# One value load of each turn issued as two loads by ranges of its rows, in a cached attention block

## The chip, the cores and the metric

The kernel runs on one core of a Trainium2 chip. The metric is the device time of one execution in microseconds (us).

## What is computed

The reference projects x to queries, attends to a cache of keys and values for every batch and head, and projects the result back. Everything is bfloat16.

```python
B, Sq, D = 8, 112, 640
H, Sk, Dh = 32, 512, 192
q = (x @ wq).reshape(B, Sq, H, Dh).transpose(0, 2, 1, 3)
scores = jnp.einsum("bhqd,bhkd->bhqk", q, k_cache) * (Dh ** -0.5)
p = softmax(scores, axis=-1)
o = jnp.einsum("bhqk,bhkd->bhqd", p, v_cache)
return o.transpose(0, 2, 1, 3).reshape(B, Sq, H * Dh) @ wo
```

## The kernel before

The work is cut into 16 turns, t = 0 to 15. A turn is one batch and one half of the heads (16 of 32): turns 0 to 7 are the first half, 8 to 15 the second. A turn has 4 steps of 4 heads each, so there are 64 steps, n = 4t + s. In step n TensorE (PE) computes the scores of n (lines 368 to 383), then the product of probabilities and values of step n - 2 (lines 459 and 470), pieces of the projection of a later batch (line 313) and of the output projection of an earlier one (line 504), and the transposes of the probabilities of step n - 1 (line 431). VectorE (DVE) takes the row maximum and the normalisation, ScalarE (ACT) the exponential and the evacuations of PSUM. The order on each engine is written out by hand in lists; a small planner (`Plan`) turns the named dependencies into waits on counting semaphores. A consumer of an operation with several semaphores waits for each of them.

All loads are issued by SyncE (SP), on one queue, in this order from turn 3 on: K(t), V(t-1, 8), in some turns a weight, V(t, 0), then K(t+1) and so on.

- `load_k` (line 143, issue at 150) loads the keys of a turn with one transposing DMA into one of two buffers, kt. It waits until the scores of turn t - 2 are done.
- `load_v` (line 157, issue at 165) loads the values of 8 heads: V(t, 0) for the heads of steps 0 and 1 of the turn, V(t, 8) for those of steps 2 and 3. One load has 128 rows, one for each partition of SBUF; a row is 8 heads of 1,536 bytes. It waits until the values that lay in its buffer have been used (`PVm`, line 470). From turn 2 on V(t, 0) goes to buffer vt1 and V(t, 8) to vt0, but for the last.
- The weights: `load_wo` (208) for the output projection in turns 2 and 3 (first half) and 10 and 11 (second half), `load_wq` (198) for the second half of the query projection in turns 5 to 8. The weight of w_of[t] stands between V(t-1, 8) and V(t, 0).

In the source, the first matmul of step n that reads the values is named `PVt` (line 464); it depends on the transposed probabilities and on the value load. The four PVt of a turn read V(t, 0) twice, then V(t, 8) twice.

Of the kernel before, what the change touches and what calls it, by code (L numbers as in the profile page):

```python
# [11 lines left out]
class Plan:  # L12
# [7 lines left out]
    def add(self, eng, name, deps, emit, sem=None, inc=1):  # L20
        assert name not in self.ops, name
        self.ops[name] = dict(eng=eng, deps=deps, emit=emit, sem=sem or eng, inc=inc)
# [30 lines left out]
def build_mha_kernel(nc, x, k_cache, v_cache, wq, wo, out):  # L53
# [16 lines left out]
    def place(n):  # L70

        return divmod(n, 4)
# [3 lines left out]
    for n in range(NN):  # L76
        t, s = place(n)
# [3 lines left out]
    with ExitStack() as es:  # L81
# [42 lines left out]
        add, order = P.add, P.order  # L124
# [6 lines left out]
        v_home = [0, 1, 2] + [i % 2 for i in range(3, len(v_units))]  # L131
# [3 lines left out]
        def v_tile(i):  # L135
            return {2: vx, 3: v_late}[v_home[i]] if v_home[i] > 1 else vt[v_home[i]]

        def v_free(i):

            old = [j for j in range(i) if v_home[j] == v_home[i]]  # L140
            return [step_of[v_units[old[-1]][0], 2 * v_units[old[-1]][1] + j] for j in range(2)] if old else []

        def load_k(t, lo, hi):
# [10 lines left out]
            for s in range(lo // 4, hi // 4):  # L154
                k_piece[t, s] = name

        def load_v(t, lo, hi):
            half, b = divmod(t, B)
            i = v_units.index((t, lo // 8))
            name = ("V", t, lo)  # L160
            deps = [("PVm", n, 1) for n in v_free(i)] + {2: [("KT", HU - 1)], 3: [("Qb", NM - 1, LP - 1)]}.get(v_home[i], [])

            def emit(e):
                src = v_cache[b, half * HU + lo:half * HU + hi].rearrange("u (r q) d -> r u (q d)", q=4)
                return e.dma_start(v_tile(i)[:, lo % 8:lo % 8 + hi - lo, :], src)
            add("SP", name, deps, emit, f"mV{v_home[i]}", 16)
            order["SP"].append(name)
            for s in range(lo // 4, hi // 4):
                v_piece[t, s] = name
# [51 lines left out]
        load_kn(8, 16)  # L221
        load_wq(0, 6)
        load_v(0, 0, 8)
        load_x(1, 2, 4)
        load_x(2, 4, 7)
        load_v(0, 8, 16)
        load_k(1, 0, HU)
        load_v(1, 0, 8)
        load_k(2, 0, HU)
        load_v(1, 8, 16)  # L230
# [617 lines left out]
def bass_standalone__mha_block_cached__near_ridge_kernel(  # L848
    nc: bass.Bass,
    x: bass.AP,  # L850
    k_cache: bass.AP,
    v_cache: bass.AP,
    wq: bass.AP,
    wo: bass.AP,
    out: bass.AP,
):
    return build_mha_kernel(nc, x, k_cache, v_cache, wq, wo, out)
# [28 lines left out]
```

## Time and profile before

| | us |
|---|---|
| time, two runs | 456.86 and 459.51, median 458.19 |
| span of the profiled execution | 456.1 |
| TensorE matmuls busy | 432.3 (95%) |
| VectorE busy | 364.6 (80%) |
| ScalarE busy | 334.1 (73%) |
| value load, median from issue to landing (30 loads, 1,536 KB each) | 8.6 |
| key load, the same (15 transposes) | 24.6 |
| wo load, the same (4 loads, 1,920 KB each) | 13.0 |

The profile is of one execution. "Busy" is the time in which an engine has an instruction at work; "idle before" is the time in which it waited, with the releaser that came last. PE is TensorE's matmuls, PEld its weight loads, SPq the instructions of SP, which are issues of DMAs: their duration is the time that SP needs to hand the DMA to the queue, not the time of the transfer. The transfers run on 16 DMA engines; "to landing" is the time from the issue to the last of their completions. Lines such as L165 are lines of the kernel.

### The profile page before, as it was taken

The numbers are of one execution on the slowest core, as the hardware profiler recorded it, in microseconds if no ns is written. First come the engines' busy times: TensorE is split into PE (matmuls) and PEld (weight loads), VectorE is DVE, ScalarE is ACT, GpSimd is POOL, SyncE is SP. The second block draws the span as 40 slices with busy tenths as digits, with TensorE's granted clock in tenths as the row PEclk, the third lists the DMA queues.
The fourth block names the chain that finished last, engine by engine and source line by source line (L and its number), as shares of the span: only waits on it lengthen the run. The fifth ranks groups of instructions, "written<-read, shape, count | busy, mean of one in ns | idle before, by whom it ended". The sixth has DMA issues, their size and how long they took to land.

```text
span 456.1 us, 14769 instructions
## 1 busy us (share of the span) xinstructions
PE 432.3 (95%) x6227; PEld 398.1 (87%) x6227; DVE 364.6 (80%) x1160; ACT 334.1 (73%) x782; POOL 0.7 (0%) x6
## 2 busy tenths in 40 slices
PE   5788999999979999999999999997999999999996
PEld 4777888989979899999999999996999999999996
DVE  0577799888868989888888888886688888889971
ACT  3668799867857777877687768776577687767783
POOL 0000000000000000000000000000000000000000
PEclk9999999999999999999999999998899999999999
DMA  8999999999999999999999999999989999999972
GB/s 266 373 363 202 284 244 374 216 314 313 245 317 230 345 230 316 243 293 276 253 319 239 315 228 334 282 235 367 226 225 262 261 213 250 270 225 251 225 204 64
DMA packets 243442, 121.93 MB, mean 267 GB/s; under 512 B 194864, under 2 KB 243376, under 8 KB 243376
## 3 DMA queue, kind: packets, MB, share of 16 engines
q1 hardware_dynamic: 243376, 120.99, 110.0%
q8 instruction: 49, 0.80, 0.7%
q14 instruction: 17, 0.14, 0.1%
HBM read 70.35 MB, written 1.15 MB: 157 GB/s over the span
## 4 chain that ended last, share of the span: by engine, by line
PE 79%; ACT 10%; DMA 6%; DVE 5%; issue 0%; SPq 0%; DVEq 0%
PE ps L504 17%; PE ps L313 16%; PE ps L470 10%; PE ps L431 9%; PE ps L381 7%; ACT p_sb L401 6%; PE ps L459 6%; PE ps L368 6%; PE ps L370 5%; DMA wo_sb<-in_wo_dram 3%; DVE s_sb L396 2%; DMA vt<-in_v_cache_dram 2%; PE ps L543 1%; ACT oT_sb L480 1%; PE ps L567 1%; DVE p_sb L405 1%
## 5 line engine op out<-in xcount | busy, mean ns | idle before, releaser
L401 ACT ACTIVATE p_sb<-s_sb,nmx 112x512 bf16<-112x512 f32 x256 | 182.4, 713 | 83.8 <-DVE s_sb L396 81.8
L396 DVE TENSOR_SCALAR_CACHE_REDUCE s_sb<-ps 112x512 f32<-112x512 f32 x256 | 167.2, 687 | 42.5 <-ACT p_sb L401 20.0
L313 PE MATMUL ps<-xT_sb,wq_sb 128*128 128x224 bf16 x960 | 111.4, 262 | 1.3 <-ACT xT_sb L278 1.3
L504 PE MATMUL ps<-oT_sb,wo_sb 128*128 128x224 bf16 x840 | 97.7, 261 | 3.3 <-DMA wo_sb<-in_wo_dram 3.3
L313 PEld LDWEIGHTS ps<-xT_sb,wq_sb 128*128 128x128 bf16 x960 | 90.2, 99 | 2.8 <-DMA wq_sb<-in_wq_dram 1.1
L405 DVE TENSOR_SCALAR p_sb<-p_sb,rinv 112x512 bf16<-112x512 bf16 x256 | 79.0, 350 | 4.4
L504 PEld LDWEIGHTS ps<-oT_sb,wo_sb 128*128 128x128 bf16 x840 | 78.8, 98 | 3.9 <-DMA wo_sb<-in_wo_dram 3.6
L319 ACT ACTIVATE qr<-ps 128x448 bf16<-128x448 f32 (+1 forms) x112 | 48.9, 441 | 16.1 <-PE ps L313 16.0
L431 PE MATMUL ps<-ident,p_sb 112*128 112x112 bf16 x944 | 57.2, 214 | 1.9 <-ACT oT_sb L480 1.9
L437 ACT ACTIVATE pT_sb<-ps 128x896 bf16<-128x896 bf16 x59 | 53.3, 903 | 4.4 <-PE ps L431 3.7
L431 PEld LDWEIGHTS ps<-ident,p_sb 112*128 112x128 bf16 x944 | 52.0, 99 | 4.1 <-ACT oT_sb L480 4.1
L470 PE MATMUL ps<-pT_sb,vt 128*128 128x112 bf16 x880 | 52.8, 213 | 0.0
L480 ACT ACTIVATE oT_sb<-ps 128x672 bf16<-128x672 f32 x64 | 45.4, 710 | 6.0 <-PE ps L470 6.0
L401 ACT ACTIVATION_READ_ACCUMULATOR p_sb<-s_sb,nmx 112x1 f32 x256 | 48.4, 189 | 0.0
L470 PEld LDWEIGHTS ps<-pT_sb,vt 128*128 128x128 bf16 x880 | 44.1, 98 | 4.3
L437 DVE COPY pT_sb<-ps 128x896 bf16<-128x896 bf16 x59 | 36.4, 616 | 9.1 <-PE ps L431 9.0
L459 PEld LDWEIGHTS ps<-pT_sb,vt 128*64 128x64 bf16 x880 | 24.0, 109 | 14.2 <-issue 9.5
L459 PE MATMUL ps<-pT_sb,vt 128*64 128x112 bf16 x880 | 32.1, 216 | 4.2 <-DVE s_sb L396 2.4
L370 PE MATMUL ps<-kt,qh 128*112 128x256 bf16 x128 | 35.2, 275 | 0.0
L368 PE MATMUL ps<-kt,qh 128*112 128x256 bf16 x128 | 35.1, 274 | 0.0
L368 PE MATMUL ps<-kt,qr 128*112 128x256 bf16 x112 | 31.0, 277 | 3.8 <-DVE qh L346 2.3
L383 PE MATMUL ps<-kt,qh 64*112 64x256 bf16 x128 | 34.0, 291 | 0.0
(70 smaller groups left out, 481.3 us busy)
## 6 DMA issues: line engine op xcount, KB each, us to landing
vt<-in_v_cache_dram SPq DMA_DIRECT2D x30, 1536.0 KB, 8.6
wo_sb<-in_wo_dram SPq DMA_DIRECT2D x4, 1920.0 KB, 13.0
wq_sb<-in_wq_dram SPq DMA_DIRECT2D x7, 960.0 KB, 11.2
wo_sb<-in_k_cache_dram SPq DMA_DIRECT2D x2, 768.0 KB, 10.2
wo_sb<-in_k_cache_dram SPq DMA_DIRECT2D x1, 1536.0 KB, 15.0
wo_sb<-in_v_cache_dram SPq DMA_DIRECT2D x1, 1536.0 KB, 7.8
wq_sb<-in_v_cache_dram SPq DMA_DIRECT2D x1, 1536.0 KB, 8.1
out_dram<-xT_sb SPq DMA_DIRECT2D x8, 140.0 KB, 2.3
```

The lines of the kernel that those rows point to most:

```text
L313: mm = e.matmul(ps[:, bank, j * S2:(j + 1) * S2], wq_sb[:, dc, c0:c0 + 128], xT_sb[:, dc, bp * S2:(bp + 1) * S2], start=(dc == 0), stop=(d ...
L368: e.matmul(ps[0:SQ, 2 * j, hs], ev, ktb[:, :, 0, cs(i)], start=(h == 0), stop=False, skip_group_check=True)
L370: mm = e.matmul(ps[0:SQ, 2 * j + 1, hs], od, ktb[:, :, 2, cs(i)], start=(h == 0), stop=False, skip_group_check=True)
L396: return e.tensor_scalar(s_sb[:, a, :].rearrange("p (e c) -> p e c", e=2), ps[0:SQ, 2 * j:2 * j + 2, h * 256:(h + 1) * 256], -scale, None, ...
L401: return e.activation(p_sb[:, k, :], s_sb[:, a, :], ACTF.Exp, bias=nmx[:, k:k + 1], scale=-1.0, accum_out=rsum[:, k:k + 1])
L405: return e.tensor_scalar(p_sb[:, k, :], p_sb[:, k, :], rinv[:, k:k + 1], None, op0=ALU.mult)
L431: mm = e.transpose(psb[:, bank, c:c + SQ], p_sb[:, (4 * n + 2 * j + h) % 8, q * 128:(q + 1) * 128], ident[0:SQ, 0:SQ])
L437: return e.activation(dst, src, ACTF.Copy) if j == 0 else e.tensor_copy(dst, src)
L459: mm = e.matmul(ps[64 * h:64 * h + 64, b0 + j, SQ:2 * SQ], vtb[:, h0 + 2 * j + h, d0:d0 + 64], pT(j, h, q), start=(q == 0), stop=(q == 3))
L470: mm = e.matmul(ps[:, b0 + j, 2 * h * SQ:(2 * h + 1) * SQ], vtb[:, h0 + 2 * j + h, d0:d0 + 128], pT(j, h, q), start=(q == 0), stop=(q == 3))
L480: return e.activation(dst.rearrange("p (j c) s -> p j c s", j=2), ps[:, b0:b0 + 2, 0:3 * SQ].rearrange("p j (c s) -> p j c s", c=3), ACTF. ...
L504: mm = e.matmul(ps[:, o_bank(u, f), j * S2:(j + 1) * S2], wo_sb[:, KU * (u % 2) + k, m * 128:(m + 1) * 128], oT_sb[:, u % NO, k, :], start ...
```

## The change

In turns 3 to 14, V(t, 0) is issued as two DMAs one behind the other: the first covers partitions 0 up to a cut, the second the rest. The cut is 120 in turns 3 to 5, 104 in turns 6 to 8, 88 in turns 9 to 11 and 72 in turns 12 to 14. The bytes, the buffer and the wait ahead of the load are the same. Each buffer's semaphore becomes one with the suffix a, and the second DMA of a split load has one of its own with the suffix b, so that PVt of the first step after such a load waits on both. V(t, 8) and the loads of turns 0 to 2 and 15 stay single. All later lines move down by 6.

```diff
+        V_ROWS = [(120, 128), (104, 128), (88, 128), (72, 128)]
+
         def load_v(t, lo, hi):
             half, b = divmod(t, B)
             i = v_units.index((t, lo // 8))
             name = ("V", t, lo)
             deps = [("PVm", n, 1) for n in v_free(i)] + {2: [("KT", HU - 1)], 3: [("Qb", NM - 1, LP - 1)]}.get(v_home[i], [])
 
+            rows = V_ROWS[(t - 3) // 3] if lo == 0 and 3 <= t < 15 else (128,)
+
             def emit(e):
                 src = v_cache[b, half * HU + lo:half * HU + hi].rearrange("u (r q) d -> r u (q d)", q=4)
-                return e.dma_start(v_tile(i)[:, lo % 8:lo % 8 + hi - lo, :], src)
-            add("SP", name, deps, emit, f"mV{v_home[i]}", 16)
+                dst = v_tile(i)[:, lo % 8:lo % 8 + hi - lo, :]
+                cuts = [0, *rows]
+                return tuple(e.dma_start(dst[r0:r1], src[r0:r1]) for r0, r1 in zip(cuts, cuts[1:]))
+            add("SP", name, deps, emit, tuple(f"mV{v_home[i]}{'ab'[j]}" for j in range(len(rows))), 16)
```

## The prediction, made before the result was known

> **What bounds the kernel now.** The page first. TensorE is busy for 95% of a span of 456.1 us, and the chain that ended last is 79% PE. The windows put PE at 26.00 of 26.00 us in most turns from 176 on, so a turn costs about 26.1 us of matmuls. What can still change the time is a load that comes so late that PE waits. The waits of PE on DMA are few in this profile:
>
> ```profile
> PE ps L504 <- DMA wo_sb<-in_wo_dram: 3.3, 1, 3.3
> PE ps L459 <- DVE s_sb L396: 2.4, 1, 2.4
> PE ps L459 <- DMA vt<-in_v_cache_dram: 1.1, 1, 1.1
> ```
>
> The first is in turn 11: the chain of waits there is one long piece, the second-half load of wo. The second, at 127.9 to 130.4, is put down to DVE, but V(3,8) was issued at 121.93 and its time to landing is 8.3 us, so it landed at 130.2 and was the real releaser. The timeline of turn 11:
>
> ```profile
> 302.57 0.58 SPq L165 DMA_DIRECT2D vt<-in_v_cache_dram  x1
> ...
> 303.20 0.58 SPq L208 DMA_DIRECT2D wo_sb<-in_wo_dram  x1
> ...
> 317.22 1.11 PE L504 MATMUL ps<-oT_sb,wo_sb 128*128 128x224 bf16 x5 [3.33 <-DMA wo_sb<-in_wo_dram]
> ```
>
> wo was issued at 303.20, with no wait of its own, as soon as K(11) and V(10,8) ahead of it were issued, and took 14.0 us to land because the DMA engines were still on what lay ahead. So the second question is whether the DMA engines have spare time. SP's timeline says how a turn goes:
>
> ```profile
> 202.41 0.37 SPq L165 DMA_DIRECT2D vt<-in_v_cache_dram  x1
> 202.82 21.18 SPq L150 DMA_TRANSPOSE kt<-in_k_cache_dram  x1
> 224.05 0.58 SPq L165 DMA_DIRECT2D vt<-in_v_cache_dram  x1
> 224.68 0.58 SPq L198 DMA_DIRECT2D wq_sb<-in_wq_dram  x1
> 228.49 0.37 SPq L165 DMA_DIRECT2D vt<-in_v_cache_dram  x1
> ```
>
> SP is held 21 us by the K transpose, then issues V(t,8), a weight, V(t+1,0) and the next K. The V loads are queued some 4 us and more before their data moves. From V(3,0) to the wo of turn 11 I found no stretch in which all the engines were out of work for want of an issue: the DMA chain is as long as PE's turn, and what is added to it adds up until PE has to wait for it. The slack of V(t,8) (issue plus time to landing, against the first L459 matmul that reads it) shows it: turn 4 2.7 us, 5 1.7, 6 2.0, 7 1.5, 8 0.4, 9 4.1, 10 1.1, 11 2.7, 12 3.7. K(t) has 3 to 6 us, V(t,0) 7 to 10 (1.3 in turn 3).
>
> The last view is DMA traffic in 157 to 161 us, 40 slices of 0.1 us, the end of V(5,0) and the start of K(6):
>
> ```profile
> DMA  9998989899989999999000000000004999999999
> GB/s 415 323 430 307 430 307 430 307 430 323 430 292 318 279 294 289 274 138 54 31 15 31 31 15 31 31 15 15 18 18 95 282 289 292 292 287 289 287 297 292
> ```
>
> V moves at some 370 GB/s and K at 290, but between them lie 1.2 us at 15 to 31 GB/s, which is one engine of sixteen at work (370/16 = 23). The transposes have begun and stand still until the last engine is through with V. So a load costs the chain what its most loaded engine takes.
>
> **The change part by part.** It touches only V(t,0), turns 3 to 14.
>
> The extra issue on SP: 12 more DMAs of 0.37 to 0.58 us. Each lies directly ahead of a K transpose whose data does not move for another 8 us or more, so the queue hides it: 0. Without that cover it would be 12 x 0.58 = 7 us.
>
> The extra wait on PE: the first matmul after V(t,0) now waits on two semaphores. The trace has no such row; bounds are 0 and the 0.18 us of issue gap that stands before many L459 loads, 12 x 0.18 = 2.2 us. In turns 3 to 10 the end is set by the DMA chain, which leaves at most 4 x 0.18 = 0.7; I take 0.4. Behind that wait are queued PE's later matmuls of the step.
>
> The rows per engine. A load of 128 rows is 1.573 MB, which at 370 GB/s is 4.25 us, 8 rows for each engine, 0.53 us for a row. No DMA of the trace has an uneven count: the loads have 128 rows (16 x 8), the stores 112 (16 x 7). Lower bound: the pieces are dealt so that no engine gets more than 8 rows, 0 us. Upper bound: each piece goes in equal shares, as all DMAs seen do, on the most engines (up to 16) that divide its rows, counted from the same first engine. Then 120+8 is 8 rows on 15 engines and 1 on 8, at most 9; 104+24 is 8 on 13 and 2 on 12, at most 10; 88+40 is 8 on 11 and 4 on 10, at most 12; 72+56 is 6 on 12 and 4 on 14, at most 10. Extra rows over 8: 1, 2, 4, 2, or 0.53, 1.06, 2.12 and 1.06 us a turn. I take the upper end, since equal shares are what every row of the trace has.
>
> [...]
>
> Where it falls. Turn 3: V(3,8) has no slack, so 0.53 goes straight to PE. Turns 4 and 5 add 1.06 to the lag, inside the slack. With turns 6, 7, 8 (1.06 each) the lag is 2.1, 3.2, 4.2 against slacks of 2.0, 1.5 and 0.4: PE loses 3.8 by turn 8. Turn 9 adds 2.12 and has 4.1 of slack. Turn 10 adds 2.12, and wo, which PE already waits for, takes the whole lag. So the loss up to there is the full sum, 3 x 0.53 + 3 x 1.06 + 2 x 2.12 = 9.0 us. In turn 11 the 2.12 meet 2.7 of slack; turns 12 to 14 load no weights, slack is 3.6 and more against 1.06: 0.
>
> Sum: 9.0 + 0.4 = 9.4 us, 456.1 to 465.5 in the span. The span is 0.8 below the lower of the two runs (456.86) and 2.1 below their median, so the forecast is 458.2 + 9.4 = 467.6 us.
>
> A stall also touches PE's clock: in the windows it is 0.55 and 0.59 from 316 to 324, after the wait for wo, and 1.00 after the 2.4 us wait of turn 3. The new stalls (0.5, 1.7, 2.1 us by my sum) are shorter than that; one of 3.5 us in turn 10 is followed by the wait for wo, which hides slow matmuls. Bounds 0 to 3 us, taken 0. [...]
>
> **The rivals.** *Nothing is added (not slower).* Rows are dealt evenly, or the engine that is late anyway is one of those relieved. The 1.2 us tail above is such an engine; with it among the relieved, 0.53 and 1.06 vanish behind it and 88+40 leaves 2 x (2.12 - 1.2) = 1.8 us: 458 to 460. It decides when the late engine carries none of the second piece. For: the tail is there in most turns, about 0.8 to 1.3. Against: 8 to 12 of 16 engines are the loaded ones, and with the late one among them the costs add. Chance 0.24.
>
> *Uneven pieces are slower by themselves.* If consecutive row blocks make two engines write to the same part of SBUF at once, the pieces run at down to half speed: up to 4.25 us more for each of 8 turns, 34 + 9 = 43 us, 501; at a third of that about 480. For: nothing in the trace, it has no such load. Against: a store of 112 rows (421 to 422 us) reads SBUF at 379 GB/s and more in its middle slices, no slower than loads of 128. Chance 0.22, mostly low in its range.
>
> [...]
>
> *Faster.* The relieved engine is the late one and K starts earlier in turns 3 to 5, by 1.2 - 0.53 each: 2 us, inside the noise. By over 2%: 0.04.
>
> **How the numbers follow.** Forecast 0.48, own range 463 to 473. Nothing added 0.24, slow pieces 0.22, faster 0.04, anything else slower 0.02. Two per cent, about what a measurement of this kernel can tell from no change, is 9.2 us, 467.4, close to the forecast itself: some 0.29 of its 0.48 lie above, since the clock, the extra waits and turn 11 can only add. Slower 0.29 + 0.22 + 0.02 = 0.53; same 0.19 + 0.24 = 0.43; faster 0.04. The range, 458 to 482, leaves out the upper half of the slow pieces, the faster cases and a little of the evenly dealt one.
>
> **What would show it.** Right: between V(t,0) and K the stretch at low GB/s grows by 0.5, 1.1 and 2.1 us by split, with more than one engine's traffic in it; PE's waits on vt appear in turns 7, 8 and 10 (line 465 then) and wo lands near 326 instead of 317. Wrong: tails unchanged (dealt evenly); first pieces that move at well under 370 GB/s (slow pieces); or the added time after turn 11, where I have none.

## The result, and the profile after

The change makes the kernel slower by a seventh: 523.54 us (two runs, 523.27 and 523.81) against 458.19, a ratio of 1.143 with an interval of 1.128 to 1.157. (Times are medians of all executions; ratios leave out those in a slower state of the chip, so that they can differ a little from the quotient of two medians.) The direction was forecast, the size was not: 65 us were added where the prediction had 9.4, and its range ended at 482.

Three lines of the page after: TensorE's row of the first part (busy time, share of the span of 521.5 us, instructions), the granted clock in 40 slices of the span, in tenths, and the chain that ended last, by engine.

```profile
PE 442.8 (85%) x6227; PEld 404.7 (78%) x6227; DVE 365.4 (70%) x1160; ACT 336.3 (64%) x782; POOL 0.7 (0%) x6
...
PEclk9999999989999999999869979998599999969999
...
PE 61%; DMA 23%; ACT 8%; DVE 4%; issue 2%; SPq 0%; DVEq 0%
```

The same 6,227 matmuls are busy 10.5 us longer (432.3 before), and the rest of the added span, 54.9 us, is idle time of TensorE. On the chain, DMA has 23% where it had 6%. TensorE, with 61% of the chain where it had 79%, no longer sets the pace of the turns. Its waits on loads, and one row (issue) of a wait for which the profile shows no releaser (total, number of waits, longest, in us):

```profile
PE ps L510 <- DMA wo_sb<-in_wo_dram: 20.5, 2, 14.0
...
PE ps L319 <- DMA wq_sb<-in_wq_dram: 11.5, 2, 10.3
PE ps L465 <- DMA vt<-in_v_cache_dram: 10.7, 4, 9.0
...
PE ps L465 <- issue: 7.3, 1, 7.3
...
PE ps L374 <- DMA kt<-in_k_cache_dram: 4.0, 2, 2.2
```

Before, wo had 3.3 us in one wait, vt 1.1, wq and kt nothing worth a line. Now weights, keys and values come late: 46.7 us on the four rows of loads. Only 10.7 of them are on value loads, and these are all on V(t,8): TensorE has no wait of over 0.4 us on a split load itself. Turn 11, by the timeline (start, duration, instruction, the wait in brackets):

```profile
348.16 0.86 SPq L214 DMA_DIRECT2D wo_sb<-in_wo_dram  x1
...
349.76 7.06 SPq L171 DMA_DIRECT2D vt<-in_v_cache_dram  x2
...
371.42 1.68 PE L510 MATMUL ps<-oT_sb,wo_sb 128*128 128x224 bf16 x8 [13.96 <-DMA wo_sb<-in_wo_dram]
```

wo is issued at 348.16 and read at 371.42, 23 us later, where it took 14.0 us before. But the trace also records each of the sixteen completions of a load. Before, those of this wo came from 315.6 to 317.2, 12.4 to 14.0 us after its issue. Now fifteen of them are in at 360.9, 12.7 us after the issue, and only the last comes at 371.4, together with the last completions of V(11,0), the split load behind it. The other long waits are alike: 6.6 us on wo in turn 3, 10.3 on wq and 9.0 on V(13,8) each end with the last one or two of sixteen completions, 7 to 8.5 us after the others and within 0.2 us of the last ones of the split load behind. Of these four waits, 39.8 us, some 34 pass after all but one or two completions are in.

A further 10.0 us of TensorE's idle time are not on loads: 7.3 in the row shown, ending at 306.66, and 2.0 and 0.7 ending at 209.35 and 238.10. They stand in the middle of a group of matmuls, ahead of an instruction that waits for no semaphore, and the kernel before has none of them. Queue q8 of the profile carries 49 packets of 16 KB of the kind "instruction". Before, they came at most 15 us apart in the turns; here 16 to 22 us pass ahead of the three stops, and each stop ends 2.3 to 2.5 us after such a packet has started. So TensorE seems to have run out of instructions, whose packets also go by DMA and came late; that is inferred and was not tested.

The windows around the longest wait and an early stretch show what all this does to a turn of 26 us (columns: window, length, busy us and instructions of PE, PEld, DVE, ACT and POOL, granted clock, DMA share, GB/s):

```profile
150.00:176.00 26.00, 24.21 (x364) 21.78 (x362) 22.97 (x75) 18.97 (x44) 0.00 (x0) 1.00 1.18 229
360.00:386.00 26.00, 14.58 (x180) 13.14 (x181) 8.65 (x26) 6.74 (x15) 0.00 (x0) 0.74 1.25 218
```

PE has 24 us of work in the first and 15 in the second, in which the granted clock is 0.74.

The DMA traffic shows the split load itself. This is 165 to 174 us, 40 slices of 0.22 us, the same place in the turn as the prediction's view of before: the end of V(5,0), split 120+8, and the start of K(6). The first line is the busy share of the 16 DMA engines in tenths, the second what they moved.

```profile
DMA  9999999999999999999999999999998204999999
GB/s 184 177 171 198 191 212 218 218 198 205 218 212 212 191 191 198 205 184 178 191 196 197 217 154 102 77 91 88 112 93 56 34 16 98 291 289 289 358 271 221
```

Over the first 23 slices, 5 us, the engines are at work without a gap and V moves at 171 to 218 GB/s; before, it was some 370. Then comes a tail of 2.4 us at 154 down to 16 (1.2 us before); at the 23 GB/s that the prediction puts down to one engine (370/16), ever fewer engines are left in it. K, behind it, goes at some 290 as it did. So the split load is slow in itself, for as long as it lasts. The packet records agree: of the 1,024 packets of 1,536 bytes that a V(t,0) consists of, 554 to 939 took over 100 ns in the five split loads whose packets stand apart from others (medians 107 to 134), at most some 50 in a single load (median 65 to 69).

The dealing to the engines is what the prediction took, in its counts. As the split loads land, the trace has, beside one update soon after the issue of each piece, 15, 13, 11 and 12 of the first piece's semaphore, by cut, and 8, 12, 10 and 14 of the second's, where a single load has 16; that each is of one engine is inferred. The packets agree: queue q1 has 243,469 where it had 243,376, 93 more, all of them of 4 bytes (1,677, before 1,584). By the prediction's counts twelve split loads have 3 x (15+8 + 13+12 + 11+10 + 12+14) = 285 completions, and twelve single ones 12 x 16 = 192: 93.

### The profile page after: what moved, and what is told of

The parts are those of the page before. It is cut to its first block, busy times and chain, and to the rows that moved or that the text cites. A ratio compares the mean times of both kernels' runs of the same rounds, so it can differ in the third digit from the quotient of the medians.

```text
span 521.5 us, 14792 instructions
## 1 busy us (share of the span) xinstructions
PE 442.8 (85%) x6227; PEld 404.7 (78%) x6227; DVE 365.4 (70%) x1160; ACT 336.3 (64%) x782; POOL 0.7 (0%) x6
## 2 busy tenths in 40 slices
DMA packets 243535, 121.93 MB, mean 234 GB/s; under 512 B 194957, under 2 KB 243469, under 8 KB 243469
## 3 DMA queue, kind: packets, MB, share of 16 engines
q1 hardware_dynamic: 243469, 120.99, 107.0%
HBM read 70.35 MB, written 1.15 MB: 137 GB/s over the span
## 4 chain that ended last, share of the span: by engine, by line
PE 61%; DMA 23%; ACT 8%; DVE 4%; issue 2%; SPq 0%; DVEq 0%
PE ps L510 14%; PE ps L319 12%; DMA wo_sb<-in_wo_dram 9%; PE ps L476 8%; PE ps L437 7%; DMA kt<-in_k_cache_dram 6%; ACT p_sb L407 5%; PE ps L387 5%; DMA wq_sb<-in_wq_dram 5%; PE ps L465 5%; DMA vt<-in_v_cache_dram 4%; PE ps L374 4%; PE ps L376 4%; DVE s_sb L402 2%; PE ps L549 1%
## 5 line engine op out<-in xcount | busy, mean ns | idle before, releaser
L319 PE MATMUL ps<-xT_sb,wq_sb 128*128 128x224 bf16 x960 | 115.3, 268 | 11.9 <-DMA wq_sb<-in_wq_dram 11.5
L510 PE MATMUL ps<-oT_sb,wo_sb 128*128 128x224 bf16 x840 | 100.6, 266 | 20.5 <-DMA wo_sb<-in_wo_dram 20.5
L319 PEld LDWEIGHTS ps<-xT_sb,wq_sb 128*128 128x128 bf16 x960 | 92.5, 101 | 14.9 <-DMA wq_sb<-in_wq_dram 11.9
L510 PEld LDWEIGHTS ps<-oT_sb,wo_sb 128*128 128x128 bf16 x840 | 80.4, 100 | 22.3 <-DMA wo_sb<-in_wo_dram 14.2
L437 PE MATMUL ps<-ident,p_sb 112*128 112x112 bf16 x944 | 58.4, 217 | 1.9 <-ACT oT_sb L486 1.9
L476 PE MATMUL ps<-pT_sb,vt 128*128 128x112 bf16 x880 | 54.6, 216 | 2.7 <-issue 2.7
L437 PEld LDWEIGHTS ps<-ident,p_sb 112*128 112x128 bf16 x944 | 53.4, 100 | 4.1 <-ACT oT_sb L486 3.8
L465 PE MATMUL ps<-pT_sb,vt 128*64 128x112 bf16 x880 | 33.1, 218 | 25.1 <-DMA vt<-in_v_cache_dram 10.7
L476 PEld LDWEIGHTS ps<-pT_sb,vt 128*128 128x128 bf16 x880 | 45.5, 99 | 7.5 <-issue 3.0
```

The costliest lines, as they stand in the source:

```text
L319: mm = e.matmul(ps[:, bank, j * S2:(j + 1) * S2], wq_sb[:, dc, c0:c0 + 128], xT_sb[:, dc, bp * S2:(bp + 1) * S2], start=(dc == 0), stop=(d ...
L437: mm = e.transpose(psb[:, bank, c:c + SQ], p_sb[:, (4 * n + 2 * j + h) % 8, q * 128:(q + 1) * 128], ident[0:SQ, 0:SQ])
L465: mm = e.matmul(ps[64 * h:64 * h + 64, b0 + j, SQ:2 * SQ], vtb[:, h0 + 2 * j + h, d0:d0 + 64], pT(j, h, q), start=(q == 0), stop=(q == 3))
L476: mm = e.matmul(ps[:, b0 + j, 2 * h * SQ:(2 * h + 1) * SQ], vtb[:, h0 + 2 * j + h, d0:d0 + 128], pT(j, h, q), start=(q == 0), stop=(q == 3))
L510: mm = e.matmul(ps[:, o_bank(u, f), j * S2:(j + 1) * S2], wo_sb[:, KU * (u % 2) + k, m * 128:(m + 1) * 128], oT_sb[:, u % NO, k, :], start ...
```

## The experiments

Times are compared with runs of the kernel before on the same chip. P, where the expectations use a letter, is the theory of place (engines that write to the same part of SBUF slow each other, the second rival of the prediction), against the prediction's own, by which only the most loaded engine counts.

**Loads alone, by shape.** A kernel in which SP issues value loads one at a time, each waiting for the one before, and stores at the end; nothing is computed. The load of rows p0 to p1 is, in short,

```python
src = v_cache[b, h:h + 8].rearrange("u (r q) d -> r u (q d)", q=4)[r0:r0 + p1 - p0]
e.wait_ge(sem, 16 * (i - 1))
e.dma_start(vt[p0:p1, :, :], src).then_inc(sem, 16)
```

> No attention is computed: SP alone loads values into one buffer, one load at a time, each after the one before has landed, twice through a list of row ranges; the output holds loaded values. In the changed kernel most packets of the split load take about 130 ns instead of 65. Theory P (place: the engines of a split load carry blocks of consecutive rows, and two engines that are 32 rows apart write to the same part of SBUF at half speed each): 128 rows about 4.2 us plus some 2 us of fixed time; 120, 112, 104, 96 and 88 rows from row 0 about 7 to 8 us plus 2; 64 rows at partitions 0-63 about 4.2 plus 2, but the same 64 rows at partitions 32-95 only 2.1 plus 2, whatever the source rows; 60 rows at 32-91 (not a multiple of 16) also 2.1 plus 2. Theory C (count: a load that does not use all sixteen engines is slow for that reason): 112, 96 and 64 rows fast everywhere (3.7, 3.2 and 2.1 plus 2), 120, 104, 88, 72 and 60 slow. Theory S (split: slowness comes of two loads in flight together): every single load here moves at 65 ns a packet, 120 rows in about 4.2 plus 2.

SP's timeline has a row for each load, so the time of a load is the distance between two starts (columns: start, time to issue, line). The list goes 128, 120, 112, 104, ... rows from partition 0 (lines 31 to 37), then 64 rows at 0, 64 rows at 32, 64 rows at 0 taken from rows 32 to 95 of the source, 64 rows at 32 taken from rows 0 to 63 (lines 38 to 41):

```profile
0.73 0.44 SPq L31 DMA_DIRECT2D vt<-in_v_cache_dram  x1
7.79 0.41 SPq L32 DMA_DIRECT2D vt<-in_v_cache_dram  x1
17.84 0.32 SPq L33 DMA_DIRECT2D vt<-in_v_cache_dram  x1
25.15 0.31 SPq L34 DMA_DIRECT2D vt<-in_v_cache_dram  x1
...
58.29 0.71 SPq L38 DMA_DIRECT2D vt<-in_v_cache_dram  x1
64.50 0.63 SPq L39 DMA_DIRECT2D vt<-in_v_cache_dram  x1
69.25 0.63 SPq L40 DMA_DIRECT2D vt<-in_v_cache_dram  x1
75.54 0.61 SPq L41 DMA_DIRECT2D vt<-in_v_cache_dram  x1
80.36 0.33 SPq L42 DMA_DIRECT2D vt<-in_v_cache_dram  x1
```

128 rows take 7.06 us, 120 rows, which are fewer, 10.05, and 112 rows 7.31. Sixty-four rows to partitions 0 to 63 take 6.21 us, the same to 32 to 95 4.75, and exchanging the source rows changes neither (6.29 and 4.82). So neither the number of rows nor the place in HBM decides, but the place in SBUF. The second pass of the list repeats this within 0.2 us for these shapes. In means of both passes, in us: 128 rows 6.9, 120 10.0, 112 7.3, 104 9.7, 96 7.3, 88 9.1, 72 7.2; second pieces 8 rows 3.1, 24 3.7, 40 5.6, 56 6.0. P had expected more of the 112 and 96 rows; these are taken up at the end of this section. The fixed 2 us of this expectation were the author's estimate; 128 rows show 6.9 - 4.25 = 2.65.

**The split by heads.** In the same turns the load is cut into two by heads, each with all 128 rows.

```diff
-                cuts = [0, *rows]
-                return tuple(e.dma_start(dst[r0:r1], src[r0:r1]) for r0, r1 in zip(cuts, cuts[1:]))
+                cuts = [0, 4, 8] if two else [0, 8]
+                return tuple(e.dma_start(dst[:, u0:u1, :], src[:, u0:u1, :]) for u0, u1 in zip(cuts, cuts[1:]))
```

> V(t,0) of turns 3 to 14 in two loads as in the change, but cut by heads: 4 heads of all 128 rows each, so sixteen engines with 8 rows each in both. Theories P and C: as before, 457 to 461 us. Theory S: as slow as the change, above 500 us.

457.94 us against 457.25, a ratio of 1.002 (0.998 to 1.006). Two DMAs for one, two semaphores, the extra wait on TensorE: all of it costs nothing that this comparison can tell. What costs is that the cut goes through the rows.

**Two shapes in which no engine has more than its share.** By the prediction's dealing 112+16 is 7 rows and 1 on each of sixteen engines, 64+64 is 4 and 4. The edit is V_ROWS.

```diff
-        V_ROWS = [(120, 128), (104, 128), (88, 128), (72, 128)]
+        V_ROWS = [(112, 128)] * 4
```

> All twelve splits 112+16: both pieces use sixteen engines and every engine has 8 rows in all, so no engine is loaded more than before. The imbalance of the prediction and theory C: 457 to 461 us. Theory P: rows lie in blocks of 7 and of 1, so several engines share a part of SBUF: 500 to 540 us. Theory S: about 520 us.

```diff
+        V_ROWS = [(64, 128)] * 4
```

> All twelve splits 64+64: sixteen engines with 4 rows each in both pieces. The imbalance and theory C: 457 to 461 us. [...]

112+16 took 486.91 us against 457.25 (1.067, 1.058 to 1.076), 64+64 490.80 (1.075, 1.065 to 1.086). By the prediction's step both should cost nothing, as each engine has its 8 rows. That step can't be the whole cause. P, with 500 to 540 for 112+16, was too high.

**Where in SBUF: 32+64+32.** Three pieces, by the same dealing sixteen engines in each, the middle one in the place that was fast alone.

```diff
+        V_ROWS = [(32, 96, 128)] * 4
...
-            add("SP", name, deps, emit, tuple(f"mV{v_home[i]}{'ab'[j]}" for j in range(len(rows))), 16)
+            add("SP", name, deps, emit, tuple(f"mV{v_home[i]}{'abc'[j]}" for j in range(len(rows))), 16)
```

> All twelve splits in three loads, rows 0-31, 32-95 and 96-127: sixteen engines with 2, 4 and 2 rows, again 8 rows an engine, cut by rows and with one load more than 64+64 (490.8 us). In the run that loads alone, 64 rows took 6.2 us a round at 0-63 and 4.8 at 32-95, and 32 rows at 0-31 3.8; with some 2.5 us fixed that is 1.3 + 2.3 + 1.3 = 4.9 us a turn against 4.4 for 128 rows and 7.5 for 64+64. Theory P (two engines 32 rows apart on one part of SBUF): 458 to 465 us. Theory S' (any cut by rows costs, more so with more pieces): 490 us or more.

481.03 us against 455.55 (1.053, 1.045 to 1.060): the least of the splits by rows, yet above what P expected. The traffic of one such load, 105 to 115 us, in slices of 0.25 us:

```profile
DMA  9999999999999999999999899999999966089999
GB/s 361 340 286 195 209 197 191 209 215 246 197 166 184 203 221 389 362 369 369 356 209 147 104 154 135 138 132 176 177 180 136 106 71 39 15 197 292 291 292 286
```

The load has a stretch at some 200 GB/s, one at 370 and one at 104 to 180; in the packet records the medians are some 125, 65 and 190 ns. That these are the three pieces, one behind the other, is inferred from their order: a packet record names no row, and the first stretch moves some 610 KB where the first piece has 393, so the pieces overlap. Alone, a load of 32 rows had seemed almost free (3.8 us); why it isn't here was not shown.

**The most loaded engine by itself.** From the kernel before, four extra DMAs of 8 rows behind each V(t,0) of turns 3 to 14, from HBM to the output in HBM, where the real stores overwrite them. By the dealing above they load the same eight engines, and they touch no SBUF.

```diff
+                    def extra(e, j=j):
...
+                        dst = out.rearrange("b s d -> s b d")
+                        return e.dma_start(dst[8 * j:8 * j + 8], src[8 * j:8 * j + 8, :, 0:D])
+                    add("SP", ("E", t, j), [("E", t - 1, j)], extra, f"mE{j}", 16)
```

> The kernel before, V(t,0) whole; behind it in turns 3 to 14 four more DMAs, each 8 rows of 8 runs of 1,280 bytes from the value cache to the output tensor in DRAM (overwritten at the end), so 8 engines get 32 packets more each and 8 none, with nothing written to SBUF. This is the prediction's step alone: a load costs what its most loaded engine takes. At 55 ns a packet it is 1.8 us a turn; by the prediction's sum turns 3 to 10 pay in full (8 x 1.8 = 14 us) and turns 11 to 14 nothing: 468 to 476 us. If the chain has room for it, or the late engine's tail hides it: 457 to 462 us. If turns 11 to 14 pay too: 480 us.

465.69 us against 455.55 (1.020, 1.013 to 1.026): 8.9 us, 5.8 to 11.9. So what the most loaded engine has more does cost the chain, at about two thirds of the price by the prediction's step (14 us); the four more issues a turn and the writes to HBM are in it too.

**Late and early turns.** The split in turns 11 to 14 alone, then in 3 to 10 alone.

```diff
-            rows = V_ROWS[(t - 3) // 3] if lo == 0 and 3 <= t < 15 else (128,)
+            rows = V_ROWS[(t - 3) // 3] if lo == 0 and 11 <= t < 15 else (128,)
```

> The change in turns 11 to 14 alone (88+40 once, 72+56 three times). The prediction put these turns at nothing, by slack of 2.7 to 3.7 us. In the loads alone the pieces cost 6.6 + 3.2 and 4.7 + 3.4 us against 4.4, so 5.4 and 3.7 us more. If slack covers it turn by turn: 458 to 464 us. If the lag adds up as it does in turns 3 to 10: 16 us and a slow clock of PE behind the waits, 472 to 482 us.

478.22 us against 455.55 (1.044, 1.035 to 1.052), some 20 us, where the prediction had 0 for these turns. The wait of turn 11 is in it, 3.3 us before, and a stop without a releaser:

```profile
PE ps L510 <- DMA wo_sb<-in_wo_dram: 11.7, 1, 11.7
PE ps L476 <- issue: 4.2, 1, 4.2
```

The time is that of the second forecast, in which the lag adds up, but the profiled run (473.78 us) shows no such lag: in turns 11 to 14 TensorE has no wait of over 0.3 us on a value or key load. Of wo's sixteen completions twelve are in by 316.4, and four come at 326.6 to 326.8, with the last of V(11,0). Its span is 471.9 us, 15.8 over the 456.1 of before: 8.4 are the longer wait for wo, 4.2 the stop, 4.6 longer matmuls, and small waits are 1.4 shorter.

> The change in turns 3 to 10 alone. The change costs 65 us, and in turns 11 to 14 alone it cost 20 us (ratio 1.044). If the two stretches add up: 45 us, 500 us. By the prediction, with the price of the pieces put right (3.6, 4.0 and 5.4 us a turn for 120+8, 104+24 and 88+40 by the loads alone): 3 x 3.6 + 3 x 4.0 + 2 x 5.4 = 34 us and a slow clock of PE behind the waits, 490 to 500 us.

504.53 us against 455.26 (1.106, 1.097 to 1.115), some 48 us. Early and late turns add up to 68, the 65 of the change within the noise.

**One shape in all twelve turns: 120+8.**

```diff
+        V_ROWS = [(120, 128)] * 4
```

> All twelve splits 120+8. Only one row more on 8 engines, but blocks of 8 rows: in the loads alone 120 rows took 7.4 us, 112 rows 4.8, 128 rows 4.4, so 120+8 costs about 3.6 us a turn, as 64+64 does (3.1; 490.8 us in the kernel) and more than 112+16 (1.2; 486.9 us). Theory P: 490 to 505 us. The imbalance of the prediction: 8 x 0.53 = 4 us, 462.

504.16 us against 455.55 (1.104, 1.091 to 1.116).

**What makes a place fast: 64 rows at each offset.** Loads alone, as in the first experiment, to partitions 0 to 63, 8 to 71 and so on to 64 to 127.

> No attention is computed: loads alone, one at a time, 64 rows each, at partitions 0-63, 8-71, 16-79 and so on to 64-127, three times; sixteen engines with 4 consecutive rows each every time, so only the place changes. If rows that lie 32 apart in the same half of the 128 share a part of SBUF, the 64 rows meet themselves in 16, 12, 8, 4, 0, 4, 8, 12 and 16 of their 16 blocks of four: of 512 packets some 512, 384, 256, 128, 0, 128, 256, 384, 512 go at about 120 ns instead of 65, a round takes 4.8 us at 32-95 and 6.2 at all others, where some engines are slow (a little less towards the middle), since the slowest engine ends the load. If place matters in another way (the half, the first rows), the curve is not symmetric about 32.

Lines 34 and 35 are offsets 24 and 32:

```profile
20.14 0.58 SPq L34 DMA_DIRECT2D vt<-in_v_cache_dram  x1
26.38 0.58 SPq L35 DMA_DIRECT2D vt<-in_v_cache_dram  x1
31.32 0.58 SPq L36 DMA_DIRECT2D vt<-in_v_cache_dram  x1
```

4.94 us at 32, 6.2 to 6.6 at every other offset. The times are what P expected, the counts of slow packets are not: instead of falling in steps towards 32 they are some 250 to 320 at every other offset, and about 30 at 32. The map of places in the next experiment doesn't explain this either.

**Which rows share a part.** Loads alone again, 16 rows of 32 packets of 1,536 bytes each (49 KB), by the dealing one row for each engine, in patterns.

> No attention is computed: after one full load, loads of 16 rows (8 in the last two) with 32 runs of 1,536 bytes each, one row for each engine, so that the partitions alone say which engines share. If a part of SBUF is four rows and the four rows 32 below them in the same half, and two engines on one part halve: rows 32, 36 ... 92 (all parts different) 32 packets at 65 ns, 2.1 us plus some 2.6 fixed; 0, 4 ... 60 and 64, 68 ... 124 and 0, 8 ... 120 (pairs 32 apart) and 0, 2 ... 30 and 32, 34 ... 62 (pairs of neighbours) 4.2 plus 2.6; rows 0 to 15 and 48 to 63 (four to a part) 8.4 plus 2.6; 24, 28 ... 84 and 16, 20 ... 76 (4 and 8 engines of 16 paired) 4.2 plus 2.6 with 128 and 256 of 512 packets slow; 8 rows 0, 4 ... 28 and 32, 36 ... 60 (eight parts, eight engines) 2.1 plus 2.6, though only eight engines work. If the number of engines or something else than the place decides, these eleven patterns do not differ in this order.

Lines 31 to 33 are rows 32, 36, ... 92; 0, 4, ... 60; 64, 68, ... 124. Lines 39 and 40 are rows 0 to 15 and 48 to 63, line 41 is 8 rows, 0, 4, ... 28:

```profile
20.09 0.68 SPq L31 DMA_DIRECT2D vt<-in_v_cache_dram  x1
24.80 0.55 SPq L32 DMA_DIRECT2D vt<-in_v_cache_dram  x1
31.20 0.55 SPq L33 DMA_DIRECT2D vt<-in_v_cache_dram  x1
...
68.93 0.34 SPq L39 DMA_DIRECT2D vt<-in_v_cache_dram  x1
78.17 0.32 SPq L40 DMA_DIRECT2D vt<-in_v_cache_dram  x1
87.48 0.78 SPq L41 DMA_DIRECT2D vt<-in_v_cache_dram  x1
92.19 0.69 SPq L42 DMA_DIRECT2D vt<-in_v_cache_dram  x1
```

Rows four apart from 32 to 92 take 4.71 us; 0 to 60 and 64 to 124, where rows lie 32 apart in the same half, 6.40 and 6.25; sixteen rows in a block 9.24 and 9.31. Median packets are 65, some 130 and 253 ns. Eight rows, 0 to 28, take the 4.71 us of sixteen. The three levels (expected 4.7, 6.8 and 11) come in the order that the expectations' map gives, in which four neighbouring rows share a part and so do rows 32 apart within one half; patterns that should pair only some of the engines had more slow packets, 265 to 306, than the map gives. So the map is an account that fits the levels; it is not shown row by row.

**The completions.** In 120+8, six of the seven weight loads ahead of a split load had their last completion some 10 us after the first, in the records of their landing; in the change itself five of seven, against at most 2.1 us in the kernel before. In 112+16, 64+64 and 32+64+32, whose pieces by the dealing all use sixteen engines, it is at most 4.3 us. Theory N in the expectations: engines that the following piece leaves out deliver theirs late, and TensorE waits for that. A small DMA on all sixteen engines ahead of the split load, or behind it, tells. Both are made from 120+8.

```diff
+            if len(rows) > 1:
+                def extra(e):
+                    src = v_cache[b, half * HU:half * HU + 1].rearrange("u (r q) d -> r u (q d)", q=4)
+                    return e.dma_start(out.rearrange("b s d -> s b d")[0:16, 0:1], src[0:16, :, 0:D])
+                add("SP", ("E", t), [("E", t - 1)], extra, "mE", 16)
```

> All twelve splits 120+8 (504.2 us, 10% over before, against 6.7% for 112+16), and one tiny DMA of 16 rows, one packet for each of the sixteen engines, from the value cache to the output in DRAM (overwritten at the end), between what is ahead on the queue (in weight turns the weight) and the two pieces. In 120+8 the last of the sixteen completions of five of the six weight loads comes 10 us after the first, about when the next K begins; in 112+16 at most 3.3 us after it. Theory N (an engine that has no part in what follows gives its last completion only when the next work reaches it): the tiny DMA is that work, weight loads complete within some 3 us of the first engine, PE's waits for wo and wq fall from 26 to some 10 us, 485 to 495 us. Theory W (the completion is stuck until the pieces are written): spread of 10 us and 500 to 508 us as without it.

510.85 us against 457.92 (1.115, 1.103 to 1.127), the completions of five of the seven weight loads still about 10 us apart. The last completion of the small DMA is as late as theirs (for turn 3 at 115.6, wo's at 115.4), so the next work does not release it.

> The same tiny DMA behind the two pieces, ahead of K. Theory N: the idle engine gets it when SP has handed over the pieces, some microseconds before K; spread of the weights' completions 3 to 8 us, 488 to 502 us. Theory W: spread of 10 us, 500 to 508 us.

508.93 us (1.112, 1.100 to 1.124). Here wq's completions are 2.2 to 2.8 us apart, and TensorE's wait on wq falls from the 10.5 us of 120+8 to 1.0, but the time does not; other waits have grown:

```profile
PE ps L516 <- DMA wo_sb<-in_wo_dram: 18.4, 2, 12.9
PE ps L471 <- DMA vt<-in_v_cache_dram: 16.3, 3, 12.0
...
PE ps L325 <- DMA wq_sb<-in_wq_dram: 1.0, 1, 1.0
```

Both long waits are again for one late completion: wo's last comes at 365.4 where fifteen are in by 358.8, and that of V(3,8), which stands ahead of a split load too, at 143.9 where fifteen are in by 135.3. So the late completions were moved, not removed. N is not supported: its time failed twice, and so did its spread with the small DMA ahead; with the small DMA behind, six of the seven spreads came out near it. What the records show is that five of seven weight loads ahead of a split load in the change, and six of seven in 120+8, were complete only when that load was; what causes it, and how many of the 65 us it costs beside the slow pieces, stays open.

**Why 112 rows are milder than 120.** After the runs the map was worked through. The author's estimate takes it that an engine goes through its rows in order, 0.53 us for each (4.25/8) if it is alone on its part, and that engines on one part share 1.15 times one engine's speed. The 1.15 is fitted. The patterns give 1.14 for pairs: a row of 49 KB takes 4 x 0.53 = 2.1 of the 4.7 us alone, so 3.7 of the 6.3 paired, and 2 x 2.1 / 3.7 = 1.14. The dealing is that of the prediction, taken to be in blocks of consecutive rows, which no record shows, but for 128 rows, where each engine is taken to have a part of its own. A load's time is this plus 2.65 us, what 128 rows take beyond 8 x 0.53.

| rows, each from 0 | 128 | 120 | 112 | 104 | 96 | 88 | 72 | 64 | 64 at 32 |
|---|---|---|---|---|---|---|---|---|---|
| rows for an engine | 8 | 8 | 7 | 8 | 6 | 8 | 6 | 4 | 4 |
| worked out, us | 6.9 | 10.0 | 7.2 | 10.0 | 7.5 | 10.0 | 7.5 | 6.3 | 4.8 |
| measured, us | 6.9 | 10.0 | 7.3 | 9.7 | 7.3 | 9.1 | 7.2 | 6.2 | 4.8 |

For the shortest loads the working is too high: it gives 4.5 us for 8, 24 and 32 rows (measured 3.1, 3.7 and 3.8) and 6.3 for 40 (5.6). By the map, with 8 rows in a block, engines e and e + 4 stand on the same part from the first row to the last, so 120 rows take 8 x 0.53 x 2 / 1.15 + 2.65 = 10.0. With 7 or 6, by the same map, the blocks run out of step with the parts, and the engines meet only some of the time. For the splits in the kernel the same working, both pieces behind one another on each engine, gives the DMA time that a turn adds to 8 x 0.53: 5.0 for 120+8 and 104+24, 5.3 for 88+40, 3.5 for 72+56, 1.8 for 112+16, 3.1 for 64+64, 1.6 for 32+64+32. The table has it for all split turns of a kernel; the growth of TensorE's busy time, from the pages, is put down to the clock (mean granted 0.951 in the change, 0.993 before):

| kernel | DMA, worked out | PE busy more | sum | measured (ratio less 1, times before) |
|---|---|---|---|---|
| the change | 56 | 10.5 | 67 | 65 |
| turns 3 to 10 | 40 | 12.0 | 52 | 48 |
| turns 11 to 14 | 16 | 4.6 | 20 | 20 |
| 120+8 | 60 | 8.0 | 68 | 47 |
| 112+16 | 21 | 9.0 | 30 | 31 |
| 64+64 | 38 | 7.9 | 45 | 35 |
| 32+64+32 | 19 | 8.8 | 28 | 24 |

Five of seven come out within 4 us. The two others are worked out too high, by 21 and 10 us; for 120+8 the loads measured alone fit better, ((10.0 - 2.65) + (3.1 - 2.65) - 4.25) x 12 = 43 and 8 for the clock. The working came after the runs, and no run was made to test it, so it is an account, not a proof. Nor does the sum know of the late completions and of the stops without a releaser, which are most of what the trace of turns 11 to 14 shows: that the sum fits there does not make its path right. Why the two are cheaper than it says stays open.

## Why the prediction was wrong

*What bounds the kernel* was read rightly in part: what is added to the loads ends in waits of TensorE, on wq, wo, V and K, wo of turn 11 among them. But the four longest waits are not a lag that has added up, as in the prediction; they end with the late completions of loads ahead of a split load, which it did not foresee, and 10.0 us are stops on no load.

*The extra issues and the extra wait*, 0 and 0.4 us: right, by the split by heads (1.002).

*The rows per engine*: the counts are right to the packet (93 more), and that the most loaded engine costs the chain is real (8.9 us for 14). **The step that failed is the price, "8 rows for each engine, 0.53 us for a row".** It took the speed of an engine in the load of 128 rows for the speed of any engine in any load. In the pieces the median packet takes 107 to 134 ns instead of 65 to 69, so that all rows cost more, not only those over 8. The splits that give every engine its 8 rows, which by this price cost nothing, cost 24 to 35 us. The pieces came to 56 us by the map, or 3 x ((7.3 + 0.5) + (7.1 + 1.0) + (6.5 + 3.0) + (4.6 + 3.3) - 4 x 4.25) = 49 by the loads alone, each less 2.65; by the price of the prediction they are 3 x (0.53 + 1.06 + 2.12 + 1.06) = 14, of which 9.0 were let count.

*Turns 11 to 14*, 0: wrong, 20 us by the run of these turns alone. In the profiled run the slack held, as no wait on V or K appears there; the time came by wo's late completions (8.4 us more of waiting), a stop of 4.2 us and longer matmuls (4.6), none of which the slack covers.

*The clock*, 0 with bounds 0 to 3: too low, 10.5 us of longer matmuls. What it had seen after the wait of 3.3 us for wo, 0.55 and 0.59 from 316 to 324 us, came here on a larger scale: around the wait of 14.0 us the clock is at 0.74 over a stretch as long as a turn, 360 to 386 us.

*The rivals.* What happened is, as far as the pieces go, "uneven pieces are slower by themselves", given 0.22. The mechanism that it names, engines on the same part of SBUF, is the account that fits the patterns best (4.7, 6.3 and 9.3 us), though not in all counts of slow packets. Its price, 43 us, took half speed for a whole load, near what 120 rows cost, but in eight turns instead of twelve and without the clock. Two things kept its chance low. "The trace has no such load" was counted against it, though an operation that the trace doesn't show has no price there at all. And the one row held against it, the store of 112 rows at 379 GB/s, was of the mildest shape of all (112 rows alone take 7.3 us, 120 take 10.0), and it reads SBUF where a load writes. "Nothing is added" fell with the first view of the traffic.

Of the signs that were named, "first pieces that move at well under 370 GB/s (slow pieces)" is what the window shows, and there is added time after turn 11.

## What to carry to other kernels

Cut a load along the free dimension, not along the partitions: in this kernel the split of the same twelve loads by heads cost nothing that could be told (1.002), by rows 5 to 14%. Alone, 128 rows took 6.9 us; of the ranges of rows from 0, those with 8 rows for an engine by the dealing took longest (120, 104 and 88 rows: 10.0, 9.7 and 9.1 us), those with 7 or 6 took 7.2 to 7.3 (112, 96 and 72 rows). When a wait on a load grows, look at all its completions: here the four longest were for the last one or two of sixteen (wo of turn 11: fifteen in at 360.9, the last at 371.4). And where a shape doesn't occur in the trace, the speed of its neighbour in the list is not its price: 120 rows, fewer bytes than 128, took 3.1 us longer.

## What was not expected of the hardware

Eight rows four apart, 0 to 28, take the same 4.7 us as the sixteen rows 32 to 92, so twice as many rows and, by the dealing, engines (12 KB in 0.53 us is 23 GB/s for each) did not slow the load. The rows 0 to 60, where the map pairs the engines, take 6.3 us: by the working a pair gets 1.15 times the speed of one engine, an estimate. And 60 rows at partition 32 take 4.3 us where the 64 rows from 0 take 6.2; by the dealing that is fifteen engines faster than sixteen, and by the map none of the fifteen shares a part. In four long waits of the change a load ahead of a split load had its last one or two completions only when that one was done, 7 to 10.5 us after the others (371.4 and 360.9 us for wo of turn 11).
